# Loading w_out once in fp32 and casting it on the vector engine, with its sums and combinations moved earlier

## The chip, the core and the metric

The kernel runs on one core of one Trainium2 chip. The metric is the device time of one execution in microseconds (us). PE is TensorE, which does the matmuls; DVE is VectorE, ACT is ScalarE, POOL is GpSimd (here it issues the loads), and SP is SyncE (here it issues transposes and stores). A profile is one execution; its span is some 1.8 us shorter than the same execution's timed value.

## The reference

```python
# attention over channels, 4 batches of 6080 rows, 256 channels
s = kn.transpose(0, 2, 1) @ qn / tau           # q and k normalised per channel
a = softmax(s)
x = (v @ a).reshape(24320, 256)
# feed-forward layer, 256 -> 2048 -> 256
h = x @ w_in
g = s * relu(h) ** 2 + b
out = g @ w_out
```

The kernel folds the attention matrix into w_in (`wa`), so that a group of 512 rows needs a product of v with `wa` (16 slices of 128 of the hidden width), a relu, a square, and a product with w_out. The constant b goes into a row constant, b times the sum of w_out over its 2048 rows. Most groups do the product with w_out as seven products of half blocks (the Winograd form of Strassen's method), which needs combinations T1, T2, T3 and N4 of the four blocks of w_out.

## The kernel before

w_out is loaded twice: once by a DMA that casts it to fp16 (`w_out16`, which the matmuls use), and once more as four fp32 pieces of 512 KB, from which the row sums and the combinations are made.

```python
load_w_in(0, NW)
load_v(0)
load_w_in(NW, Dff)
po(nc.gpsimd.dma_start(out=w_out16, in_=w_out_rows))       # casts on the way
load_v(1)
load_v(2)
# ... s and b ...
for i in range(NPIECE):                                    # 4 pieces
    w32 = qk_pool.tile([P, 4, C], FP32, tag="qk", name="w32")
    po(nc.gpsimd.dma_start(out=w32, in_=w_out_rows[:, ts(i, 4), :]))

def rowconst_sum(i):
    if i < NPIECE - 1:
        po(nc.vector.tensor_add(acc, w_pieces[0] if i == 0 else acc, w_pieces[i + 1]))
    else:                                                  # then 512 and 256 wide
        ...
def combine_w(i):                                          # per piece, on DVE
    po(nc.vector.tensor_sub(T1[:, part, :], B12, B11))
    po(nc.vector.tensor_sub(B12, B22, B12))
    po(nc.vector.tensor_add(B11, B11, B12))
    po(nc.vector.tensor_sub(N4[:, part, :], B21, B11))
def cast_w(i):                                             # per piece, on ACT
    po(nc.scalar.copy(out=T2[...], in_=w[:, 0, :, :P]))
    po(nc.scalar.copy(out=T3[...], in_=w[:, 0, :, P:]))
```

This work is laid on steps of the main loop; a step is one of the 16 slices of a group, so step 17 is the second slice of group 1. Each engine takes its instructions in the order of the program. The hidden values stand in two PSUM tiles (`ps_h`), which a relu frees, and the relus write to two buffers (`rpool`), which a square frees:

```python
for s in range(NS + FT):
    g, m = divmod(s, FT)
    mm1(g, m)                                   # PE: v with wa
    ...                                         # PE: products with w_out of an earlier group
    if m % 2 == 1: relu(g, m // 2)              # ACT
    square(...)                                 # DVE, some on ACT
    for f in side.pop(s, []): f()               # the sums, combinations and casts above
```

## Time and profile before

| | before |
|---|---|
| timed, first three runs | 732.61 us median (732.19 to 734.1) |
| span of the profile | 731.8 us; this execution was timed at 733.57 us |
| PE idle from 44 to 80 us | 3.3 us, nearly all of it from 62 to 72 |

From the page of the kernel before: the busy time of PE (and its share of the span), then busy tenths in 40 slices and the granted clock in tenths (9 is 90% or more), and last the loads of the fp32 pieces (count, size, median us from issue to landing).

```profile
PE 705.4 (96%) x7618; PEld 509.6 (70%) x7618; DVE 624.6 (85%) x873; ACT 537.8 (73%) x574; POOL 83.5 (11%) x159
...
PE   4798999999999999999999999999999999999997
...
DVE  4759999988888989898888989998888888888886
...
PEclk9999999999999999999999999999999999999999
...
w<-in_moe_w_out_dram POOLq DMA_DIRECT2D x4, 512.0 KB, 14.8
```

PE is busy in every slice after the load phase, and the stages read below all have a granted clock of 1.00, so time can only come out of the few microseconds in which PE stands. The prediction finds them between 62 and 72 us and shows the lines.

### The profile page before, as it was taken

Reading aid. Unit: us, or ns where it says so; the run is one execution under the profiler, and the core shown is the slowest. Engines: PE = TensorE matmul, PEld = TensorE weight load, DVE = VectorE, ACT = ScalarE, POOL = GpSimd, SP = SyncE. Lnnn points to the kernel's source line nnn. Section 1 sums busy time; section 2 is a strip of 40 time slices with the busy share of each in tenths; the row PEclk is TensorE's granted clock in tenths of the full one; section 3 lists DMA queues with packets and bytes.
Section 4 is the critical chain, followed back from the end, with each engine's and each line's share of the span. In section 5 each row is a group of like instructions: output and inputs, shape, how many; then the busy total and the mean of one; then the engine's idle time right before and its main releaser. Section 6 shows DMA issues by size and latency. Waiting matters only on the chain.

```text
span 731.8 us, 17840 instructions
## 1 busy us (share of the span) xinstructions
PE 705.4 (96%) x7618; PEld 509.6 (70%) x7618; DVE 624.6 (85%) x873; ACT 537.8 (73%) x574; POOL 83.5 (11%) x159
## 2 busy tenths in 40 slices
PE   4798999999999999999999999999999999999997
PEld 2555777776777777776677777777668777777776
DVE  4759999988888989898888989998888888888886
ACT  5468877778777777787777777777877777777772
POOL 4532220001121110001010210000000000000000
PEclk9999999999999999999999999999999999999999
DMA  9999998236487664333667685323233333321201
GB/s 236 209 246 134 213 183 120 65 88 126 91 133 167 125 98 98 88 73 67 137 117 143 118 147 126 70 64 68 77 77 80 87 75 73 96 59 58 67 30 74
DMA packets 83664, 80.61 MB, mean 110 GB/s; under 512 B 55712, under 2 KB 58592, under 8 KB 83584
## 3 DMA queue, kind: packets, MB, share of 16 engines
q0 software_dynamic: 23536, 40.51, 33.2%
q1 hardware_dynamic: 59616, 37.64, 20.6%
q8 instruction: 60, 0.98, 0.6%
q10 hardware_dynamic: 432, 1.31, 0.5%
q14 instruction: 20, 0.16, 0.1%
HBM read 81.00 MB, written 24.90 MB: 145 GB/s over the span
## 4 chain that ended last, share of the span: by engine, by line
PE 84%; DMA 6%; ACT 4%; DVE 3%; issue 1%; POOL 1%; POOLq 0%; DVEq 0%; ACTq 0%
PE h_ps L537 40%; PE o_ps L679 37%; PE s_ps L142 4%; ACT r L547 2%; DMA w<-in_moe_w_out_dram 2%; DMA qk<-in_q_dram 2%; PE wa_ps L274 1%; DMA w_in<-in_moe_w_in_dram 1%; DMA qk<-in_k_dram 1%; ACT g L558 1%; DVE g L560 1%; ACT L247 1%; POOL qk L126 1%; PE o_ps L585 0%; DVE S L605 0%
## 5 line engine op out<-in xcount | busy, mean ns | idle before, releaser
L547 ACT ACTIVATE r<-h_ps 128x1024 f16<-128x1024 f32 (+1 forms) x384 | 388.7, 1015 | 162.7 <-PE h_ps L537 158.6
L537 PE MATMUL h_ps<-vT,wa 128*128 128x512 f16 (+7 forms) x1632 | 452.5, 364 | 5.8 <-ACT r L547 4.3
L679 PEld LDWEIGHTS <-S 128*128 128x128 f16 x2944 | 198.1, 98 | 86.6 <-issue 1.5
L679 PEld LDWEIGHTS <-g 128*128 128x128 f16 x2208 | 155.0, 98 | 74.0
L560 DVE TENSOR_TENSOR g<-r 128x2048 f16<-128x2048 f16 (+2 forms) x154 | 176.9, 1149 | 22.1 <-ACT r L547 21.7
L679 PE MATMUL o_ps<-T,S 128*128 128x128 f16 x2208 | 183.5, 219 | 1.2 <-DVE S L605 0.7
L537 PEld LDWEIGHTS <-wa 128*128 128x128 f16 x1632 | 136.5, 98 | 27.0 <-issue 6.2
L679 PE MATMUL o_ps<-w_out,g 128*128 128x128 f16 x1472 | 134.2, 219 | 0.0
L565 DVE SCALAR_TENSOR_TENSOR o_sb<-o_ps,s_out,u 128x256 f32<-128x256 f32 x138 | 66.5, 482 | 51.2 <-PE o_ps L679 49.3
L558 ACT ACTIVATE g<-r 128x1024 f16<-128x1024 f16 x92 | 96.9, 1053 | 0.0
L320 POOL DMA_DIRECT2D v<-in_v_dram x48 | 25.8, 538 | 517.2 <-DMA vT<-v 333.0
L142 PE MATMUL s_ps<-qk 128*128 128x256 f16 (+1 forms) x384 | 69.7, 281 | 14.3 <-ACT qk L133 7.1
L565 DVE SCALAR_TENSOR_TENSOR u<-o_ps,s_out,rowconst 128x256 f32<-128x256 f32 x138 | 66.0, 479 | 2.8 <-PE o_ps L679 1.6
L679 PE MATMUL o_ps<-N,g 128*128 128x128 f16 x736 | 63.5, 219 | 0.0
L679 PE MATMUL o_ps<-w_out,S 128*128 128x128 f16 x736 | 63.4, 219 | 0.0
L165 ACT ACTIVATE sq<-qk 128x1024 f16<-128x1024 f16 (+3 forms) x49 | 50.4, 1033 | 10.6 <-DMA qk<-in_k_dram 7.5
L607 DVE TENSOR_TENSOR S<-S,g 128x2048 f16<-128x2048 f16 x46 | 56.3, 1224 | 1.3
L611 DVE TENSOR_TENSOR S<-g,S 128x2048 f16<-128x2048 f16 x46 | 56.0, 1217 | 0.0
L605 DVE TENSOR_TENSOR S<-g 128x2048 f16<-128x2048 f16 x46 | 55.9, 1216 | 0.0
L609 DVE TENSOR_TENSOR S<-g 128x2048 f16<-128x2048 f16 x46 | 55.9, 1215 | 0.0
L142 PEld LDWEIGHTS <-qk 128*128 128x128 f16 (+1 forms) x384 | 32.6, 101 | 20.2 <-DVE qk L132 9.0
L162 DVE TENSOR_TENSOR sq<-qk 128x1024 f16<-128x1024 f16 (+3 forms) x49 | 33.1, 675 | 2.7 <-DMA qk<-in_q_dram 2.7
(67 smaller groups left out, 279.4 us busy)
## 6 DMA issues: line engine op xcount, KB each, us to landing
out_dram<-o_sb SPq DMA_DIRECT2D x46, 512.0 KB, 3.0
v<-in_v_dram POOLq DMA_DIRECT2D x47, 256.0 KB, 3.8
qk<-in_k_dram POOLq DMA_DIRECT2D x42, 256.0 KB, 7.0
qk<-in_q_dram POOLq DMA_DIRECT2D x42, 256.0 KB, 8.2
vT<-v SPq DMA_TRANSPOSE x182, 2.8
w<-in_moe_w_out_dram POOLq DMA_DIRECT2D x4, 512.0 KB, 14.8
raw<-in_q_dram ACTq DMA_DIRECT2D x2, 512.0 KB, 6.6
raw<-in_k_dram SPq DMA_DIRECT2D x2, 512.0 KB, 7.0
```

The lines of the kernel that those rows point to most:

```text
L142: po(nc.tensor.matmul(self.s_ps[:, ch, :], kc[:np_, j, ts(ch, P)], qc[:np_, j, :], start=(c == 0 and j == 0 and ch == 0), stop=(c == len(s ...
L165: po(nc.scalar.activation(out=st["sq"][:np_, 1, js, :], in_=kc[:np_, js, :], func=AF.Square))
L537: po(nc.tensor.matmul(dst, wa[:, ci, ts(m, P)], src, start=(ci == 0), stop=(ci == CH - 1), skip_group_check=True))
L547: po(nc.scalar.activation(out=r16[:, :, i % 2, :n], in_=h_tiles.pop((g, i))[:, :, :n], func=AF.Relu))
L558: po(nc.scalar.activation(out=dst, in_=src, func=AF.Square))
L560: po(nc.vector.tensor_mul(dst, src, src))
L565: po(nc.vector.scalar_tensor_tensor(out=dst, in0=src, scalar=s_out, op0=ALU.mult, in1=add, op1=ALU.add))
L605: po(nc.vector.tensor_add(S[1], A21, A22))
L607: po(nc.vector.tensor_sub(S[2], S[1], A11))
L609: po(nc.vector.tensor_sub(S[3], A11, A21))
L611: po(nc.vector.tensor_sub(S[4], A12, S[2]))
L679: po(nc.tensor.matmul(st[name][:, j, :], a()[:, i, ts(j, P)], w[:, i, :], start=first, stop=last, skip_group_check=True))
```

## The change

The intent is to read w_out from memory once. The casting load goes; the four fp32 pieces are loaded earlier, ahead of v(2); DVE casts them to `w_out16` at steps 6 to 9; and, as the pieces are there earlier, row sums, row constant and combinations move forward by one or two steps. ACT's casts of T2 and T3 are spread out.

```diff
--- before.py
+++ after.py
@@ -371,21 +371,20 @@
     load_v(0)
     load_w_in(NW, Dff)
     w_out_rows = moe_w_out.rearrange("(fo p) d -> p fo d", p=P)
-    po(nc.gpsimd.dma_start(out=w_out16, in_=w_out_rows))
     load_v(1)
+
+    NPIECE = FT // 4
+    w_pieces = []
+    for i in range(NPIECE):
+        w32 = qk_pool.tile([P, 4, C], FP32, tag="qk", name="w32")
+        po(nc.gpsimd.dma_start(out=w32, in_=w_out_rows[:, ts(i, 4), :]))
+        w_pieces.append(w32)
     load_v(2)
     s_bc = consts.tile([P, 1], FP32)
     po(nc.gpsimd.dma_start(out=s_bc, in_=moe_s.to_broadcast((P, 1))))
     b_bc = consts.tile([P, 1], FP32)
     po(nc.gpsimd.dma_start(out=b_bc, in_=moe_b.to_broadcast((P, 1))))
     s_out = consts.tile([P, 1], FP32)
-
-    NPIECE = FT // 4
-    w_pieces = []
-    for i in range(NPIECE):
-        w32 = qk_pool.tile([P, 4, C], FP32, tag="qk", name="w32")
-        po(nc.gpsimd.dma_start(out=w32, in_=w_out_rows[:, ts(i, 4), :]))
-        w_pieces.append(w32)
 
     g0.start()
     NCH0 = len(g0.chunks)
@@ -445,6 +444,9 @@
         po(nc.vector.tensor_add(B11, B11, B12))
         po(nc.vector.tensor_sub(N4[:, part, :], B21, B11))
 
+    def cast_w_out(i):
+        po(nc.vector.tensor_copy(out=w_out16[:, ts(i, 4), :], in_=w_pieces[i]))
+
     def cast_w(i):
         w = w_pieces[i].rearrange("p (i h) c -> p h i c", h=2)
         po(nc.scalar.copy(out=T2[:, ts(i, 2), :], in_=w[:, 0, :, :P]))
@@ -461,12 +463,14 @@
         at_step(max(0, i // 2 * 4 - 1) + i % 2, f)
     at_step(14, lambda: po(nc.vector.tensor_scalar_mul(
         out=s_out, in0=s_bc, scalar1=1.0 / (LAM * LAM))))
+    for i in range(NPIECE):
+        at_step(6 + i, lambda i=i: cast_w_out(i))
     for i in range(NPIECE + 1):
-        at_step(11 + i, lambda i=i: rowconst_sum(i))
-    at_step(23, rowconst_mm)
+        at_step(10 + i, lambda i=i: rowconst_sum(i))
+    at_step(21, rowconst_mm)
     for i in range(NPIECE):
-        at_step(16 + 2 * i, lambda i=i: combine_w(i))
-        at_step(21 + 2 * i, lambda i=i: cast_w(i))
+        at_step(14 + 2 * i, lambda i=i: combine_w(i))
+        at_step(22 + 3 * i, lambda i=i: cast_w(i))
     for g in range(NG):
         if g >= 3:
             at_step(max(g - 4, 0) * FT + 2, lambda g=g: load_v(g))
```

## The prediction

> **What bounds the kernel now.** I read the page first. PE is busy 96% of the span, every slice after the second is at 9 tenths, and PEclk is 9 throughout, so only PE idle time can be won. The table by stages says where that idle time lies (columns: stretch, length, busy time and instruction count of PE, PEld, DVE, ACT, POOL, then granted clock, DMA share, GB/s):
>
> ```profile
> span 731.8 us, 17840 instructions
> ...
> 44.00:60.00 16.00, 16.00 (x107) 10.09 (x108) 11.70 (x18) 10.58 (x12) 3.99 (x7) 1.00 1.04 255
> 60.00:62.00 2.00, 2.00 (x14) 1.26 (x13) 1.86 (x6) 2.00 (x5) 0.00 (x0) 1.00 1.33 163
> 62.00:64.00 2.00, 1.44 (x11) 0.91 (x10) 1.90 (x5) 2.00 (x4) 0.00 (x0) 1.00 1.48 96
> 64.00:66.00 2.00, 1.88 (x12) 0.96 (x11) 1.86 (x6) 1.92 (x5) 0.00 (x0) 1.00 1.56 46
> 66.00:68.00 2.00, 1.00 (x6) 0.46 (x5) 2.00 (x4) 0.66 (x3) 0.93 (x2) 1.00 0.66 53
> 68.00:70.00 2.00, 1.09 (x6) 0.58 (x6) 2.00 (x3) 2.00 (x3) 2.00 (x5) 1.00 0.84 124
> 70.00:72.00 2.00, 1.38 (x11) 0.73 (x9) 1.44 (x3) 1.64 (x2) 1.85 (x4) 1.00 0.93 149
> ...
> 80.00:200.00 120.00, 119.47 (x1303) 85.97 (x1301) 108.66 (x154) 93.49 (x100) 13.34 (x25) 1.00 0.68 122
> ```
>
> PE loses 0.56 + 0.12 + 1.00 + 0.91 + 0.62 = 3.2 us between 62 and 72, nothing from 44 to 60, and about 2 us in all of 80 to 700 (rows of the same table). The other 21 us are the load phase of the first 44 us, which the change leaves alone as the loads ahead of w_out keep their order, and the drain at the end. So 3.2 us, 0.4% of the time, is the ceiling of any gain here.
>
> The chain of waits and the timeline tell what fills 62 to 72 (start, duration, what; in brackets the idle time before it and its releaser):
>
> ```profile
> 41.12 13.53 DMA w<-in_moe_w_out_dram
> ```
>
> ```profile
> 47.80 0.74 DVE L269 TENSOR_SCALAR wa<-wa_ps,rs 128x512 f16<-128x512 f32 x1
> 53.35 1.23 DVE L428 TENSOR_TENSOR acc<-w,w 128x1024 f32<-128x1024 f32 x1 [2.44 <-DMA w<-in_moe_w_out_dram]
> 58.34 0.68 DVE L560 TENSOR_TENSOR g<-r 128x1024 f16<-128x1024 f16 x1
> 66.13 0.48 DVE L436 TENSOR_SCALAR rowconst<-rc_ps,b_bc 128x256 f32<-128x256 f32 x1
> 66.53 1.22 DVE L560 TENSOR_TENSOR g<-r 128x2048 f16<-128x2048 f16 x1
> ```
>
> ```profile
> 59.12 1.02 ACT L547 ACTIVATE r<-h_ps 128x1024 f16<-128x1024 f32 x1 [1.09 <-DVE g L560]
> 67.84 1.02 ACT L547 ACTIVATE r<-h_ps 128x1024 f16<-128x1024 f32 x1 [1.34 <-DVE g L560]
> ```
>
> ```profile
> 62.66 0.59 PE L537 MATMUL h_ps<-vT,wa 128*128 128x512 f16 x2 [0.56 <-ACT r L547]
> 68.91 1.02 PE L537 MATMUL h_ps<-vT,wa 128*128 128x512 f16 x4 [1.91 <-ACT r L547]
> ```
>
> The four fp32 pieces of w_out land late. DVE stands 2.44 us before its first row sum, then works without a pause through sums and combinations, and the square of group 1 that stands behind them (66.53) comes late. ACT's relu waits for that square because its r buffer (two of them) is not free, and PE waits for the relu because its h_ps bank (two) is not. DVE's backlog, not bandwidth, is the immediate limit.
>
> **What the Trainium skill says.** "VectorE: DVE Perf Modes", section "The perf-mode tier table", has an fp32 copy run at twice the rate of an fp32 two-operand addition. The trace agrees: a 128x1024 cast from fp32 takes 0.69 us (the raw casts of the first chunks), the row sum of that size 1.23 us. "DMA: Bandwidth & Descriptors", section "Issuing engines are not separate DMA queues", says that all queues share 16 engines and interleave. The trace fits: the v transposes, normally 2.8 us to landing, take up to 15.3 us, and the loader's next v waits until 67.07. Shortening that queue helps them. "Perfetto Trace Analysis", section "Optimization Strategy", says to find the gaps in the regime of interest and what they wait for; that is the reading above.
>
> **The change part by part.** I call the 16 f-slices of a group steps; step s is the s-th pair of L537 matmuls.
>
> *DMA, removed.* The casting load of w_out (1 MB of fp16) goes. Its predecessor w_in landed at 40.2, it landed at 31.28 + 14.6 = 45.9: 5.7 us of the queue. The pieces move in front of v(2), after v(1). Estimate: v(1) lands at 40.2 + 1.25 = 41.5 (q and k loads of its size come in pairs every 2.5 us); a piece takes about 1.5 us (the third landed at 41.12 + 13.53 = 54.65, the fourth at 46.44 + 9.7 = 56.1), so the four land at 43, 44.5, 46 and 47.5; v(2) at about 48.7, where it was (its transposes were issued at 48.08). So v(2) pays nothing, and the pieces come 8 us earlier.
>
> *DVE, added.* Four casts of 0.69 us; consecutive ones of this size start 0.61 apart, so 2.44 us. By the order of the instructions they stand behind the square of 46.27 (cast 0), behind the next square (cast 1), behind the wa scaling that was at 47.80 (cast 2) and behind the g square that was at 49.31 (cast 3); row sums follow one step sooner, combinations two steps sooner, and the last square of group 0 (58.34 before) now stands behind the first combination. Nothing waits for DMA any more.
>
> *DVE replayed*, with the start-to-start times of the trace (1.15 to 1.26 for a row sum, 0.61 for the 512-wide one, 0.33 for the 256-wide one, 1.71 for the four of a combination, 0.61 for a square): 46.27 square, 46.88 cast, 47.49 square, 48.10 cast, 48.71 wa, 49.37 cast, 49.98 vT copy, 50.59 square, 51.20 cast, 51.81 sum, 52.97 square, 53.58 and 54.84 sums, 55.98 square, 56.59, 57.20 and 57.31 the small ones, 57.64 first combination, 59.35 last square of group 0 (ends 60.04), 59.96 to 65.1 three combinations, 65.1 rowconst, 65.5 the square that was at 66.53. So DVE ends this stretch 1.0 us earlier, although 2.44 us were added: the 2.44 us stand and the smaller ones are filled. But one square, the last of group 0, is 1.0 us later.
>
> *PE and ACT replayed.* (a) The wa scaling ends at 49.45 rather than 48.54. It frees the bank of the second output tile, whose first matmul came near 49.14: a wait of about 0.4 us. (b) The relu at 59.12 waits for the last square and moves to 60.13; PE's step 24 goes from 60.21 to 61.2, step 26 from 62.66 to 63.67. PE is 1.0 us behind here, (a) included. (c) Then it regains: the square of 66.53 ends at 66.7 rather than 67.75, but before the waiting relu ACT has one more relu (65.4, after PE's step 27 at 64.76) and two casts of T (0.3 apart) to do, so it starts at 66.98 rather than 67.84, and PE's long wait ends at 68.05 rather than 68.91. (d) ACT's last pair of T casts (0.66 us) now falls after that, in the shadow of PE's b=1 matmuls; the next relus come at 68.84 and 70.37, before 69.70 and 70.6. PE's first seven-product step starts at 70.99 rather than 71.85. From there PE is the bound in both, and the lead is kept to the end.
>
> The sum: minus 1.0 us up to step 26, plus 1.85 us after it: 0.85 us gained. 732.6 - 0.85 = 731.7 us.
>
> **The rivals.** (1) The chain puts 13.53 us on the w_out pieces, so taking 5.7 us of DMA off the queue could look like 5.7 us of the span. Against it: PE was never idle while they flew; at most the 3.2 us of 62 to 72 can go. If my replay is too strict in ACT's casts, 729.5. (2) DVE becomes the bound: its work from 44 to 72 grows by 2.44 us and its idle time from 44 to 60 was 16 - 11.7 = 4.3. If the recovery in (c) does not come because ACT's later casts or a landing of vT hold PE, only (a) and (b) stay: 733.6. (3) w_out's pieces, now needed at step 11 (48.92), come late: the first cast is done by 47.6, and only slices 0 to 3 need it; the fourth is needed at step 23, near 59, and done by 52. A landing would have to slip by over 3 us; then 734 or more. (4) The row constant's fp32 matmul, two steps earlier, blocks PE in order if the last sum is late: by the ledger the sum ends at 57.7 and PE arrives near 58.3, so it does not, but 0.6 us is a thin margin.
>
> **Range and chances.** The ceiling is 3.2 us, and the losses foreseen come to 1.0 to 1.5 us. With a spread of the runs of before of 732.19 to 734.1 (two of three within 0.4), I take 729.8 to 733.8. Two per cent is 14.7 us, which neither direction can reach by any route in the trace: faster 0.01, same 0.98, slower 0.01.
>
> **What would show it.** The w_out load gone from the DMA issues; no wait of DVE on w between 44 and 60; DVE at over 15 of 16 us in 44 to 60; four casts in 46.9 to 52; a relu waiting for a square until about 60.1; PE's step 26 later than 62.66 and its long wait ending near 68, not 68.9; the same PE idle time after 80. I am wrong if PE waits for w_out, if PE's wait at step 32 ends later than 68.9 (then the time rises), or if it vanishes (then the gain is 2 us or more).

## The result, and the profile after

The changed kernel takes 732.66 us (median of 6 runs, 732.52 to 732.96); before took 732.70 us in the same rounds (6 runs, 732.19 to 734.38). The ratio is 0.9995, with a 95% interval of 0.9982 to 1.0008. Ratios here are the mean time of one kernel's fast runs over that of the other's in the same rounds, so they are not quite the ratio of the medians quoted. The time is the same at the 2% threshold, and the interval does not exclude no difference at all.

The profiled span is 730.8 us, 1.0 us less than the profile of before. The difference between a clear 1.0 us in the spans and nearly nothing in the medians is the main thing that the prediction did not foresee, and the experiments start with it.

The page of the changed kernel, same rows as before:

```profile
PE 706.2 (97%) x7618; PEld 510.1 (70%) x7618; DVE 626.5 (86%) x877; ACT 537.5 (74%) x574; POOL 82.3 (11%) x158
...
w<-in_moe_w_out_dram POOLq DMA_DIRECT2D x4, 512.0 KB, 11.3
```

PE's busy time is the same within 0.2%, and a piece takes 11.3 us to land instead of 14.8. The table by stages (stretch, length, busy time and count of PE, PEld, DVE, ACT, POOL, then clock, DMA share, GB/s):

```profile
44.00:60.00 16.00, 15.81 (x103) 9.77 (x104) 14.81 (x25) 9.75 (x11) 2.39 (x5) 1.00 1.08 180
60.00:62.00 2.00, 1.61 (x12) 1.01 (x11) 1.90 (x5) 1.92 (x3) 0.46 (x1) 1.00 0.37 49
62.00:64.00 2.00, 1.43 (x10) 0.78 (x9) 1.86 (x6) 2.00 (x5) 1.06 (x2) 1.00 0.51 94
64.00:66.00 2.00, 2.00 (x14) 1.27 (x13) 1.93 (x5) 1.75 (x4) 0.63 (x2) 1.00 0.93 119
66.00:68.00 2.00, 1.75 (x11) 0.94 (x10) 2.00 (x4) 2.00 (x5) 1.71 (x4) 1.00 1.11 206
68.00:70.00 2.00, 1.38 (x7) 0.61 (x7) 1.32 (x2) 2.00 (x4) 0.31 (x1) 1.00 1.09 191
70.00:72.00 2.00, 2.00 (x20) 1.36 (x19) 2.00 (x3) 2.00 (x4) 1.37 (x3) 1.00 0.79 115
...
80.00:200.00 120.00, 119.47 (x1303) 85.93 (x1301) 108.62 (x156) 93.18 (x99) 11.70 (x22) 1.00 0.60 113
```

PE now stands 0.19 us between 44 and 60, and 0.39 + 0.57 + 0.25 + 0.62 = 1.8 us between 60 and 72, instead of 3.2. DVE's busy time from 44 to 60 rose from 11.7 to 14.8 us; PE's and DVE's in the row of 80 to 200 are the same within 0.04. DVE in the timeline (start, duration, what): the first of the four casts, the first row sum, the last square of group 0, the row constant, and the square of group 1 that stands behind all of them.

```profile
46.93 0.69 DVE L448 CAST w_out<-w 128x1024 f16<-128x1024 f32 x1
...
51.80 1.22 DVE L427 TENSOR_TENSOR acc<-w,w 128x1024 f32<-128x1024 f32 x1
...
59.30 0.68 DVE L564 TENSOR_TENSOR g<-r 128x1024 f16<-128x1024 f16 x1
...
65.04 0.48 DVE L435 TENSOR_SCALAR rowconst<-rc_ps,b_bc 128x256 f32<-128x256 f32 x1
65.43 1.22 DVE L564 TENSOR_TENSOR g<-r 128x2048 f16<-128x2048 f16 x1
```

No line has a wait in brackets: DVE has an unbroken queue from 46.3 to 69.1, where before it stood 2.44 us for the pieces. ACT's relus of the same stretch:

```profile
60.08 1.02 ACT L551 ACTIVATE r<-h_ps 128x1024 f16<-128x1024 f32 x1 [1.65 <-DVE g L564]
...
66.86 1.02 ACT L551 ACTIVATE r<-h_ps 128x1024 f16<-128x1024 f32 x1
```

The first starts when the square of 59.30 ends (59.98), 1.0 us later than before. The second, whose counterpart started at 67.84, is 1.0 us earlier. It has no wait: ACT was busy with a cast of T until then, and the square had ended some 0.2 us before. So DVE and ACT were ready almost together. PE's waits:

```profile
61.15 0.59 PE L541 MATMUL h_ps<-vT,wa 128*128 128x512 f16 x2 [0.39 <-ACT r L551]
...
63.62 0.59 PE L541 MATMUL h_ps<-vT,wa 128*128 128x512 f16 x2 [0.57 <-ACT r L551]
...
67.94 1.02 PE L541 MATMUL h_ps<-vT,wa 128*128 128x512 f16 x4 [0.25 <-ACT r L551]
```

Step 26 starts at 63.62 (before 62.66), but the long wait of step 32 ends at 67.94 (before 68.91).

### The profile page after: what moved, and what is told of

It is laid out like the page before. It is cut to its first block, busy times and chain, and to the rows that moved or that the text cites. A ratio compares the mean times of both kernels' runs of the same rounds, so it can differ in the third digit from the quotient of the medians.

```text
span 730.8 us, 17839 instructions
## 1 busy us (share of the span) xinstructions
PE 706.2 (97%) x7618; PEld 510.1 (70%) x7618; DVE 626.5 (86%) x877; ACT 537.5 (74%) x574; POOL 82.3 (11%) x158
## 4 chain that ended last, share of the span: by engine, by line
PE 85%; ACT 6%; DVE 4%; DMA 4%; issue 1%; POOL 0%; ACTq 0%; POOLq 0%; DVEq 0%
PE h_ps L541 41%; PE o_ps L683 37%; PE s_ps L142 4%; ACT r L551 3%; DMA qk<-in_q_dram 2%; PE wa_ps L274 2%; DMA raw<-in_q_dram 1%; ACT g L562 1%; DVE g L564 1%; PE o_ps L589 1%; ACT L247 1%; ACT sq L165 1%; DVE acc L427 0%; ACT L222 0%; DVE w_out L448 0%
## 5 line engine op out<-in xcount | busy, mean ns | idle before, releaser
L569 DVE SCALAR_TENSOR_TENSOR o_sb<-o_ps,s_out,u 128x256 f32<-128x256 f32 x138 | 66.3, 480 | 51.6 <-PE o_ps L683 49.6
## 6 DMA issues: line engine op xcount, KB each, us to landing
w<-in_moe_w_out_dram POOLq DMA_DIRECT2D x4, 512.0 KB, 11.3
```

What stands on the lines that cost most here:

```text
L569: po(nc.vector.scalar_tensor_tensor(out=dst, in0=src, scalar=s_out, op0=ALU.mult, in1=add, op1=ALU.add))
```

## The experiments

All ran with five rounds against the kernel before, except the third look, which is one execution. "The square" below is the square of group 1 that started at 66.53 in the first profile of before and at 65.43 in the changed kernel. My theory (A1 in the expectations) is that DVE's queue up to that square sets when PE gets going again at step 32, and that what stands before what within the queue does not matter.

### The kernel before, again

No edit. The question: is the profile of before typical of it?

> The kernel before, unchanged, as a control: the two profiled spans were 731.8 and 730.8 us, but the two medians 732.70 and 732.66. Theory A (the ledger: the change saves 0.9 to 1.0 us in every execution): this kernel's profile again has a span of 731.6 to 732.0 us, DVE waits 2.4 us for the first row sum, PE's long wait ends at 68.9, and the timed runs scatter around 732.6. Rival B (the kernel before has executions of more than one length, and the profile was taken in a long one): the profile differs from the first by 0.5 us or more, by a different landing of the w_out pieces or of vT.

Measured: span 731.2 us; timed 733.06 us (732.49 to 733.88, 5 runs) against 732.92 (731.61 to 733.64, 9 runs) of the same kernel, ratio 1.0005 (0.9991 to 1.0019). DVE's first row sum in this profile:

```profile
52.77 1.22 DVE L428 TENSOR_TENSOR acc<-w,w 128x1024 f32<-128x1024 f32 x1 [1.91 <-DMA w<-in_moe_w_out_dram]
```

It started 0.58 us earlier than in the first profile (53.35), and the span is 0.6 us shorter. Rival B holds: the kernel before has no single length. The ledger (the prediction's account of the gain, worked out from the first profile) started from one draw. The profiled execution was timed at 733.57 us, 1.0 us above the median of 732.61. Where the record lists a clock for the executions of before (33 of them), 23 are at 0.999 or more, as the profiled one was, and none of these took longer than 733.55.

### The kernel before, a third look

No edit. This asks whether the span follows the landing of the pieces one to one. Theory E is that the landing of the pieces holds the kernel before, one to one.

> The kernel before, unchanged, a third profile. Theory E: its span differs from the other two by as much as its first row sum is later or earlier: span = 731.2 + (start of the first row sum - 52.77), within 0.15 us.

```profile
52.20 1.23 DVE L428 TENSOR_TENSOR acc<-w,w 128x1024 f32<-128x1024 f32 x1 [1.39 <-DMA w<-in_moe_w_out_dram]
```

The formula gives 731.2 + (52.20 - 52.77) = 730.63; the span was 730.7 us. So in three profiles the first row sum started at 53.35, 52.77 and 52.20, and the spans were 731.8, 731.2 and 730.7 us. The third execution of before was as short as the changed kernel. Timed runs of before (39, on more than one chip) lie from 731.61 to 734.42 us with a median of 733.06. The longest were not profiled, and that they too are late landings is not shown. There is a rival: of the 33 whose clock is on record, the 10 at 0.997 or 0.998 took 733.44 to 734.42 us, the other 23 took 731.61 to 733.55. A lower clock may be what lengthens those ten.

The three profiles also show where the landing differs. The queue holds v(2), then s and b (0.5 KB each), then the pieces. v(2) had landed when its transposes were issued, at 48.08, 47.86 and 47.91; b landed at 50.7, 50.1 and 49.6 (its issue plus its time to landing), and the first piece 1.3 us later in each. So the difference arises while s and b are in front. Why they take 1.7 to 2.6 us is open.

### The changed kernel, again

No edit.

> The changed kernel, unchanged. Theory A: span 730.7 to 731.0 us, PE idle between 60 and 72 of 1.8 us, ratio to before 0.998 to 0.9995 with five rounds. Rival B: the span is the same, but the ratio's interval includes 1, because most executions of before are shorter than the profiled one.

Measured: span 730.7 us; 732.64 us (732.48 to 732.84, 5 runs), ratio 0.9997 (0.9984 to 1.0009). Its waits are those of the first profile within 0.1 us. All 11 timed runs of the changed kernel lie within 0.5 us (732.48 to 732.96), where 39 of before spread over 2.8 us, or the 23 at a clock of 0.999 or more over 1.9 us. (The next two kernels, without the wait too, each have one long run in five, 734.04 and 733.79, both at 0.998, which suggests that not all of the scatter comes from the pieces.) The theory that the change saves 0.9 to 1.0 us in every execution falls. What it does is to take the landing of the pieces off the path: they are there before DVE asks for them (they landed from 42.4 to 46.8 us; the first cast starts at 46.93).

### Combinations one step later

```diff
-        at_step(14 + 2 * i, lambda i=i: combine_w(i))
+        at_step(15 + 2 * i, lambda i=i: combine_w(i))
```

This puts the last square of group 0 in front of the first combination and so removes the late relu that my sum charged with 1.0 us.

> The changed kernel with the four combinations one step later, so that the last square of group 0 stands in front of the first combination. Theory A1 (DVE's end sets the lead, what stands in front of what within the stretch does not matter at the end): the relu at 60.08 moves to about 58.5, PE's waits near 61.1 and 62.6 shrink by 0.5 to 1 us together, but the square of 65.43 stays, PE's wait at step 32 grows by as much, and the span changes by less than 0.3 us. Rival A2 (the late relu costs the end 1.0 us, as my sum had it): span 729.8 to 730.2 us.

Measured: span 730.9 us; 732.73 us (732.65 to 734.04), ratio 1.0002 (0.9989 to 1.0014). PE's waits at steps 24 and 26 are gone, and the wait at step 32 is

```profile
67.99 1.02 PE L541 MATMUL h_ps<-vT,wa 128*128 128x512 f16 x4 [1.43 <-ACT r L551]
```

It was 0.25 us and is 1.43 us, and ends at the same time within 0.05. The relu before it, which had no wait in the changed kernel, now waits for the square:

```profile
66.91 1.02 ACT L551 ACTIVATE r<-h_ps 128x1024 f16<-128x1024 f32 x1 [1.08 <-DVE g L564]
```

A1 holds: winning back the 1.0 us that PE lost up to step 26 does not move the end. ACT was free earlier, but DVE was not, and the two had been level within some 0.2 us.

### The old steps

```diff
-        at_step(10 + i, lambda i=i: rowconst_sum(i))
-    at_step(21, rowconst_mm)
+        at_step(11 + i, lambda i=i: rowconst_sum(i))
+    at_step(23, rowconst_mm)
-        at_step(14 + 2 * i, lambda i=i: combine_w(i))
-        at_step(22 + 3 * i, lambda i=i: cast_w(i))
+        at_step(16 + 2 * i, lambda i=i: combine_w(i))
+        at_step(21 + 2 * i, lambda i=i: cast_w(i))
```

> The changed kernel with the row sums, the row constant, the combinations and the T casts back at their old steps (11, 23, 16, 21); only the single load and the DVE casts stay. Theory A1: DVE works without a pause either way, the square of 65.43 stays within 0.2 us, ACT's last T casts no longer lie after it; span 730.4 to 730.9 us. Rival C (the earlier steps are what saves the time): span 731.5 us or more.

Measured: span 730.8 us; 732.63 us (732.54 to 733.79), ratio 1.0000 (0.9987 to 1.0012). The square starts at 65.52. The third part of the change, the earlier steps, is worth nothing measurable: as DVE never waits there, the two orders of its work that were tried come to the same.

### The casts twice

```diff
         po(nc.vector.tensor_copy(out=w_out16[:, ts(i, 4), :], in_=w_pieces[i]))
+        po(nc.vector.tensor_copy(out=w_out16[:, ts(i, 4), :], in_=w_pieces[i]))
```

> The changed kernel with each of the four DVE casts of w_out done twice: 4 x 0.61 = 2.44 us more on DVE, nothing else. Theory A1 (DVE's unbroken queue from 46.3 on sets when PE gets going again): the square of 65.43 moves to 67.9, PE's wait at step 32 ends near 70.2 rather than 67.94, span 732.9 to 733.3 us. Rival D (DVE has room there, and the change gains by the smaller DMA traffic alone): span under 731.5 us.

Measured: span 733.9 us; 735.69 us (735.46 to 735.81), ratio 1.0033 (1.0020 to 1.0045). On DVE, the first pair of casts, the instruction after it, and the square:

```profile
47.13 0.69 DVE L448 CAST w_out<-w 128x1024 f16<-128x1024 f32 x1
47.85 0.69 DVE L449 CAST w_out<-w 128x1024 f16<-128x1024 f32 x1
48.46 0.69 DVE L565 TENSOR_TENSOR g<-r 128x1024 f16<-128x1024 f16 x1
...
68.56 1.22 DVE L565 TENSOR_TENSOR g<-r 128x2048 f16<-128x2048 f16 x1
```

The second cast overwrites what the first wrote and starts 0.72 us after it; the next, unrelated instruction starts 0.61 after that. So the added cast costs 0.72 where my estimate had 0.61: 4 x 0.72 = 2.9 us, and the square moved by 68.56 - 65.43 = 3.1 us, of which 0.2 is that the queue began later (47.13 rather than 46.93). The span rose by 3.1 us. The size in my expectation was off by that overlap; the slope is one to one. Rival D falls: DVE has no room there.

### The casts on ACT

```diff
-        po(nc.vector.tensor_copy(out=w_out16[:, ts(i, 4), :], in_=w_pieces[i]))
+        po(nc.scalar.copy(out=w_out16[:, ts(i, 4), :], in_=w_pieces[i]))
```

> The changed kernel with the four casts of w_out on ACT at the same steps, 1.04 us each. Theory A1 foresees the square of 65.43 some 1.5 to 2.4 us earlier, as DVE is relieved; but ACT, which feeds the relus one after the other there, holds PE by up to 2 us between 48 and 52, so the span is 730.5 to 731.8 us, no clear gain. If ACT's idle time (6.2 us between 44 and 60) takes them up freely, 729.5 us.

Measured: span 731.3 us; 733.26 us (733.20 to 733.41), ratio 1.0000 (0.9987 to 1.0014). The time is as expected, but not for the reason given: I had the square 1.5 to 2.4 us earlier. On DVE:

```profile
51.40 0.69 DVE L564 TENSOR_TENSOR g<-r 128x1024 f16<-128x1024 f16 x1 [1.43 <-ACT r L551]
...
65.78 1.22 DVE L564 TENSOR_TENSOR g<-r 128x2048 f16<-128x2048 f16 x1
```

The square starts 0.35 us later, not earlier. The casts delayed ACT's relus, DVE waited for them (1.17 and 1.43 us in this stretch), and the time taken off DVE came back as waiting. PE stood 1.6 us there (at 51.42, behind a relu). Here, moving work to an engine that feeds the queue did not shorten the queue.

### Row sums from the fp16 w_out

```diff
-            po(nc.vector.tensor_add(acc, w_pieces[0] if i == 0 else acc, w_pieces[i + 1]))
+        n = 8 >> i                                   # acc is now an fp16 tile
+        src = w_out16 if i == 0 else acc
+        po(nc.vector.tensor_add(acc[:, :n], src[:, :n], src[:, n : 2 * n]))
...
-        po(nc.tensor.matmul(rc_ps, ones32, acc[:, 0, :], start=True, stop=True))
+        po(nc.tensor.matmul(rc_ps, ones16, acc[:, 0, :], start=True, stop=True))
```

> The changed kernel with the row sums taken from the fp16 w_out that the casts wrote, as a tree in fp16: about 2.3 us of DVE rather than 4.85. Theory A1: the square of 65.43 comes 2.5 us earlier, PE's waits at steps 24 and 26 go, and ACT's relus with the T casts between them become the limit: span 729.5 to 730.0 us. Rival D: no change, 730.6 to 731 us.

Measured: correct; span 729.5 us; 730.99 us (730.88 to 731.32), ratio 0.9970 (0.9957 to 0.9982). The square:

```profile
63.70 1.22 DVE L562 TENSOR_TENSOR g<-r 128x2048 f16<-128x2048 f16 x1
```

It is 1.7 us earlier, not 2.5. From the last cast to the first combination DVE took 55.85 - 51.46 = 4.4 us, where the changed kernel took 57.59 - 51.19 = 6.4, so 2.0 us were saved and not 2.5; and the whole queue began 0.26 us later in this profile (first cast at 47.19, not 46.93). The span gained 1.3 us, not the square's 1.7: the relu before step 32 starts at 65.52, right behind ACT's casts of T and 0.6 us after the square has ended, so ACT is the limit there. PE's waits at steps 24 and 26 went, as expected. Rival D falls.

### Everything from the fp16 w_out

The row sums as in the last run, and the combinations taken from `w_out16` in four instructions of 128x1024; T2 and T3 are written in fp16 at once, so ACT's casts fall away.

```diff
-        w = w_pieces[i].rearrange("p (i h) c -> p h i c", h=2)
+        w = w_out16.rearrange("p (i h) c -> p h i c", h=2)
...
+        out, a, b, op = [(T1, B12, B11, nc.vector.tensor_sub), (T3, B22, B12, nc.vector.tensor_sub),
+                         (T2, B11, T3, nc.vector.tensor_add), (N4, B21, T2, nc.vector.tensor_sub)][i]
+        po(op(out, a, b))
-        at_step(14 + 2 * i, lambda i=i: combine_w(i))
-        at_step(22 + 3 * i, lambda i=i: cast_w(i))
+        at_step(15 + 2 * i, lambda i=i: combine_w(i))
```

> Row sums and also the four combinations from the fp16 w_out, four instructions of 128x1024 in fp16 (0.69 us each) rather than sixteen of 128x256, and written in fp16 at once, so that ACT's eight T casts fall away: some 7 us of DVE and 2.6 us of ACT less than the changed kernel between 52 and 70. Theory A1: PE's idle time from 60 to 72 falls from 1.8 to under 0.6 us, what remains is a relu behind another on ACT; span 728.5 to 729.3 us, faster than both. Rival D: 730.6 to 731 us. The outputs may differ slightly, as the combinations are taken of rounded values.

Measured: correct; span 728.8 us; 730.58 us (730.47 to 730.69), ratio 0.9963 (0.9951 to 0.9976). The square now waits for ACT, and DVE is no longer the limit:

```profile
61.26 1.23 DVE L554 TENSOR_TENSOR g<-r 128x2048 f16<-128x2048 f16 x1 [1.41 <-ACT r L541]
```

PE's idle time from 60 to 72 is 0.59 us.

### The kernel before with its loads in another order

```diff
-    load_v(2)
-    # ... s and b ...
     for i in range(NPIECE):
         w32 = qk_pool.tile([P, 4, C], FP32, tag="qk", name="w32")
         po(nc.gpsimd.dma_start(out=w32, in_=w_out_rows[:, ts(i, 4), :]))
         w_pieces.append(w32)
+    load_v(2)
+    # ... s and b ...
```

This is the kernel before, w_out still loaded twice, with the pieces ahead of v(2) and of s and b.

> The kernel before with nothing changed but the order of its loads: the four fp32 pieces stand ahead of v(2), s and b, behind the casting load and v(1). No DVE work is added or moved. Theory E (the kernel before is held by the landing of the pieces, one to one): the first row sum starts at 50.8 rather than 53.3 (or 52.8 as in the control), the square of 66.53 at 64.0, and the span falls to 729.7 us, as with the fp16 sums, lower than the change under study. If v(2), now 5 us later, brings its transposed tile after 66.6, PE waits for that at step 32 and the span is 730.3 to 731.5 us. Rival F (earlier landing is only worth something together with the single load): span 731 us or more.

Measured: span 729.1 us; 730.96 us (730.83 to 731.15) against 733.55, ratio 0.9969 (0.9955 to 0.9982). DVE's first row sum and the square, and then PE's wait at step 32:

```profile
50.74 1.22 DVE L427 TENSOR_TENSOR acc<-w,w 128x1024 f32<-128x1024 f32 x1
...
63.78 1.22 DVE L559 TENSOR_TENSOR g<-r 128x2048 f16<-128x2048 f16 x1
```

```profile
66.23 1.02 PE L536 MATMUL h_ps<-vT,wa 128*128 128x512 f16 x4 [0.32 <-ACT r L546]
```

The row sum waits for nothing, the square is 2.75 us earlier than in the first profile, and v(2) does not come too late. Theory E holds. The span is 0.6 us below my figure. By the ratio the kernel gains 2.3 us (1.3 to 3.3) by moving six lines; without the runs of before at a clock of 0.997 or 0.998 it would be 1.9. So the landing of the pieces was worth some 2 us. No run moved only s and b, so what share is theirs and what is v(2)'s is not separated.

The change under study, whose pieces land earlier still (42.4 to 46.8 against 47.8 to 51.8), gave most of it back. The clean comparison is with "The old steps", which has the same steps as this run and differs in the casting load against the casts on DVE: its square starts at 65.52 against 63.78, and its span is 730.8 against 729.1. The casts cost 1.7 us, less than their 2.44, as they also fill three short waits of DVE (0.22, 0.17 and 0.22 us).

### w_out loaded once by the casting DMA

The other way to load it once: from "everything from the fp16 w_out", take out the four fp32 loads and DVE's casts, and put the casting load back.

```diff
+    po(nc.gpsimd.dma_start(out=w_out16, in_=w_out_rows))
     load_v(1)
-    for i in range(NPIECE):
-        w32 = qk_pool.tile([P, 4, C], FP32, tag="qk", name="w32")
-        po(nc.gpsimd.dma_start(out=w32, in_=w_out_rows[:, ts(i, 4), :]))
-        w_pieces.append(w32)
-    for i in range(NPIECE):
-        at_step(6 + i, lambda i=i: cast_w_out(i))
```

> The other way to load w_out once: the casting load of the kernel before stays, the four fp32 pieces are never loaded, and sums and combinations are taken from the fp16 w_out as in the run with everything from fp16. Against that run DVE has 2.44 us less (no casts) and PE's 0.2 us wait at step 11 goes; the wait at step 34 behind ACT's relu stays. Theory: span 728.4 to 728.8 us, ratio to before 0.994 to 0.996.

Measured: correct; span 728.6 us; 730.43 us (730.05 to 730.46) against 733.55, ratio 0.9959 (0.9947 to 0.9972). The only wait of PE over 0.2 us left between 45 and 76:

```profile
67.56 0.59 PE L521 MATMUL h_ps<-vT,wa 128*128 128x512 f16 x2 [0.59 <-ACT r L531]
```

This version beats the kernel before by 0.4%. It needs less of everything: one load, no casts of w_out on DVE or ACT, and combinations in well under half the DVE time. But sums and combinations are taken from rounded values, and the size of the error is not on record.

## Why the prediction was right or wrong

The predicted 731.7 us was 1.0 us from the measured 732.66, well inside the range, and the chances were right. The gain was not: 0.85 us foreseen, 0.04 by the medians and some 0.4 by the ratio, neither clear of noise. By its own steps:

**What bounds the kernel.** Right, but for small readings: the page has one 8 among the 9s of PE after the second slice, and a last slice of 7, and DVE paused 0.15 us once more for a piece (54.73). PE's busy time from 80 to 200 us is 119.47 or 119.48 us in every profile taken; what moved, moved before.

**The DMA part.** Right. The pieces landed from 42.4 to 46.8 (43 to 47.5 estimated), before DVE asked for each, and v(2) landed where it had been: its transposes were issued at 47.94 (48.08 before). One reading was off: the longest v transpose, 15.3 us, was issued at 74.5, when no piece was in flight; the eight from 48 us on took 8 to 14 us. These did gain from the shorter queue: the last of them landed at 60.5 us instead of 68.2.

**The DVE ledger.** Right nearly to the rounding: the last square of group 0 at 59.30 (ledger 59.35), the row constant at 65.04 (65.1), the square at 65.43 (65.5). DVE's busy time from 44 to 60 was 14.8 us, and I had said over 15.

**PE and ACT.** In (a) PE waited 0.19 us where about 0.4 was foreseen. Steps (b) to (d) came out within 0.15 us: the relu at 60.08 (60.13), step 26 at 63.62 (63.67), the relu at 66.86 (66.98), step 32 at 67.94 (68.05), the first seven-product step at 70.87 (70.99).

**The sum.** Right in total for the first profile (0.85 us predicted, 1.0 us in the span), wrong in what its terms mean. "Minus 1.0 us up to step 26" reads as a loss that could be won back; moving the combinations took it away and the end did not move. PE, early or late, had to wait for the square anyway.

**The size against the timed runs.** This is the step that failed, "732.6 - 0.85": a gain worked out from an execution timed at 733.57 was taken off a median of 732.6, as "two of three within 0.4" was read as noise of the timing. From its own execution, 733.57 - 0.85 = 732.72, the replay comes within 0.1 of the measured 732.66. The term "the four fp32 pieces of w_out land late" has no fixed size. In three profiles the first row sum started at 53.35, 52.77 and 52.20, and the spans followed. Mine was the latest of the three. Against their mean, (731.8 + 731.2 + 730.7) / 3 = 731.2 us, the changed kernel's 730.8 gains 0.4 us, which is what the ratio of 0.9995 says of 732.7 us.

**Rivals.** (1) failed as argued: removing 5.7 us of DMA was not 5.7 us of time. (2) was half right: DVE is the bound, as the doubled casts showed, but it was the bound before too, once the pieces had landed, and in the changed kernel ACT stood level with it. (3) and (4) did not happen: PE waited neither for w_out nor for the row constant's matmul, which started at 58.43.

So a real gain, earlier data worth some 2 us (731.2, the mean of the three looks, to 729.1 when only the loads were reordered), was mostly spent on casts on the engine that was the limit: 2.4 us of work, of which 1.7 reached the end.

## What to carry to other kernels

When a late load holds an engine that then works without a pause, look first at the order of the loads: here that alone was worth 0.3%, and a change that frees the load but adds work to the same engine gave most of it back. A replay of the engines' queues from the trace's own start-to-start times can be right to one or two tenths of a microsecond and still misjudge the gain if the profile it starts from is one draw of a kernel that waits for DMA; compare the profiled execution's own time with the median, take a second profile, or look at the spread of the runs, before predicting less than half a per cent. A delay counts only if it moves the last thing that the stretch waits for.

## What the Trainium skill lacked or had wrong

- No page has it: the landing of the same queued loads moves by over a microsecond between executions of one kernel (three profiles, from more than one chip). The first row sum that waits for them started at 53.35, 52.77 and 52.20 us, and the span moved with it (731.8, 731.2, 730.7 us); with the wait gone, the 11 runs of the changed kernel lay within 0.5 us. The differences arose while two loads of 0.5 KB stood in front of them, which landed 1.7 to 2.6 us after the load before.
- "DMA: Bandwidth & Descriptors", section "Bandwidth", gives rates by size and says nothing of casting loads. From 40 to 44 us, where the kernel before had its casting load in flight and the changed kernel mostly the uncast pieces, the profile counts 205 and 401 GB/s. But the casting load's 1 MB of fp16 took 5.7 us of the queue, and so did the four uncast pieces with 2 MB (the loads before them landed at 40.2 and 41.1, they at 45.9 and 46.8): both read the same fp32 w_out in the same time, so casting on the way neither saved nor cost queue time.
- "VectorE: DVE Perf Modes", section "The DRAIN you can't avoid", gives no start-to-start time that tells a dependent neighbour from an unrelated one. Here an instruction started 0.60 to 0.61 us after one of 0.69 us when the two were unrelated, and 0.72 us after it when it overwrote the first's output ("The casts twice") or read it (the first row sum from fp16 behind the last cast, 51.46 and 52.18).
